# Routed attention and a mixture of experts on one core: the order of the first pair's preparation

## The chip, the core and the metric

The kernel runs on one core of a Trainium2 chip. The core has five engines, each with its own queue that it works through in order: TensorE (PE in the profile, its weight loads PEld), VectorE (DVE), ScalarE (ACT), GpSimd (POOL) and SyncE (SP), which here only starts transfers. ScalarE and GpSimd can start transfers too. Transfers run on 16 DMA engines of the core. SBUF is the working memory; TensorE writes into the banks of PSUM, and VectorE and ScalarE copy results out of them. The metric is the device time of one execution in microseconds; of several executions the median counts.

## What is computed

First attention for 4 batches of 8 heads, 768 tokens and 64 columns a head. Every row of q and k is given to the nearest of 16 centroids of its head, by cosine, and a query sees only the keys with its own centroid. Then a router sends each of the 3072 rows of the attention's output to one of 8 experts, a two-layer network.

```python
q_assign = np.argmax(np.einsum('bhsd,hcd->bhsc', q_n, c_n), axis=-1)
k_assign = np.argmax(np.einsum('bhsd,hcd->bhsc', k_n, c_n), axis=-1)
mask = q_assign[:, :, :, None] == k_assign[:, :, None, :]
scores = np.where(mask, scale * np.matmul(q, k.transpose(0, 1, 3, 2)), -1000000000.0)
attn = softmax(scores)
x = rows_of(np.matmul(attn, v))          # (3072, 512)
logits = xn @ en.T / tau
out[mask_e] = gate_w[mask_e, None] * (np.maximum(x[mask_e] @ w1[e], 0.0) @ w2[e])
```

Here `q_n`, `k_n`, `c_n`, `xn` and `en` (from `expert_emb`) are rows divided by their norm.

## The kernel before

**Tiling.** Two heads of one batch are a pair; there are 16 pairs. A pair has 12 units: two halves of the queries (384 columns) by six blocks of 128 keys. A unit is `scores` (L347 to L361), `expo` (L363 to L366) and `attend` (L368 to L396). `scores` is four matrix products for the two heads into one PSUM tile `s_ps`, of which there are two: first the H part, bf16 one-hot rows of the centroids (`kH` against `qH`, scaled by 2 to the 60th, so that only keys of the query's centroid survive the exponential), then the T part, the float32 rows themselves (`kT` against `qT`). The two parts add up in PSUM. `expo` takes the exponential on ScalarE, which frees the `s_ps` tile. `attend` multiplies with v on TensorE and adds up the denominators on VectorE (`acc`).

**Preparation of a pair.** `prep_pieces` (L228) gives seven pieces. `turn0` and `turn1` transpose one half of q and one of k on TensorE, three 128 by 128 blocks each, into a PSUM bank of `misc` (two banks); ScalarE copies q out (L246, with the scale), VectorE copies k out (L248). `products` multiplies both with the centroids `cnB` (L254) and ScalarE copies the result to `asT` (L262). `assign` turns that (L267); VectorE takes the maximum (L275) and compares (L276), and GpSimd weighs the matches (L277). `choose` (L283, L284) makes one-hot rows `oh` on VectorE. `hots` turns them (L297) and copies them out as `qH` (VectorE, L303) and `kH` (ScalarE, L306); with k's turn goes a small product with `vs` (L320). `values` (L313 to L315) makes `vs`, sums over v, on GpSimd.

**Order.** Inside one block (from L840) the order of TensorE, VectorE and ScalarE is that in which the program is written; the other engines, and what stands ahead of the block, are ordered by the framework's scheduler. In the block all seven pieces of pair 0 come first, then scores and exponentials of units 0 and 1. Then the loop takes two units a round: scores and exponentials of the two units after, then `between` (L798), which puts one piece of the next pair at each of the six rounds `it` of half a pair, then the two attends, and every sixth unit `total` (L397), the sums of the denominators.

**The beginning.** `load` (L136) starts two transfers of 192 KB for each of q, k and v of a pair, all from SP's queue. ScalarE's queue starts those of the centroids, of the experts' rows `emb` and of `tau`. Ahead of the block stand memsets and small constants, then the centroids: `unit_rows` (L194) takes a Square and a Sqrt on ScalarE and two small VectorE instructions; the rows are scaled (L207), turned (L209) and copied to `cnB` (L212). The experts' rows go the same way (L219 to L224) to `embT`, which is first read when the first batch is routed. Pair 1's `turn0` comes in the first round of the loop, its `turn1` after the first two attends (L878).

Of the kernel before, what the change touches and what calls it, by code (L numbers as in the profile page):

```python
# [9 lines left out]
F32 = mybir.dt.float32  # L10
BF16 = mybir.dt.bfloat16
I32 = mybir.dt.int32
ALU = mybir.AluOpType
ACTF = mybir.ActivationFunctionType
# [4 lines left out]
P = 128  # L19
# [18 lines left out]
def kernel(  # L38
# [12 lines left out]
    nc = tc.nc  # L51

    B, H, S, D = q.shape
    C = centroids.shape[1]
    E, DM = moe_expert_emb.shape
# [4 lines left out]
    HS = S // 2  # L60
# [8 lines left out]
    KD = DM // P  # L69
# [15 lines left out]
    ident = const.tile([P, P], F32, name="ident")  # L85
    identb = const.tile([P, P], BF16, name="identb")
    cnB = const.tile([P, NHP, 2 * C], F32, name="cnB")
    embT = const.tile([P, KD, 2 * C], F32, name="embT")
# [3 lines left out]
    epsc = const.tile([P, 1], F32, name="epsc")  # L92
# [22 lines left out]
    smp = ctx.enter_context(tc.tile_pool(name="smp", bufs=2))  # L115
# [14 lines left out]
    def misc():  # L130
        return psM.tile([P, 512], F32, tag="misc", name="misc")
# [1 line left out]
    pairs = [(b, hp) for b in range(B) for hp in range(NHP)]  # L133
    ld = {}

    def load(n, names):  # L136
        b, hp = pairs[n]
        t = ld.setdefault(n, {})
        for nm in names:
            t[nm] = ldp.tile([P, NJ, 2, D], F32, tag=nm + "32", name=nm + "32")  # L140
            for h in range(2):
                nc.sync.dma_start(
                    out=t[nm][:, :, h],
                    in_={"q": q, "k": k, "v": v}[nm][b, 2 * hp + h].rearrange(
                        "(p j) d -> p j d", j=NJ
                    ),
                )

    c_sb = smp.tile([P, D], F32, name="c_sb", bufs=1)
    emb = smp.tile([E, DM], F32, name="emb", bufs=1)  # L150
    tau = smp.tile([E, 1], F32, name="tau", bufs=1)
    load(0, "qkv")
    nc.scalar.dma_start(out=c_sb, in_=centroids.rearrange("h c d -> (h c) d"))
    nc.scalar.dma_start(out=emb, in_=moe_expert_emb)
    nc.scalar.dma_start(out=tau, in_=moe_tau.to_broadcast([E, 1]))


    make_identity(nc, ident)
# [32 lines left out]
        for t in range(2):  # L191
            nc.gpsimd.memset(oh[:, :, 2 * t : 2 * t + 2, :, C : C + 1], (-1.0, 1.0)[t])

    def unit_rows(dst, src, n):  # L194

        junk = smp.tile([P, DM], F32, tag="junk", name="junk")
        nc.scalar.activation(
            junk[0:n, 0 : src.shape[1]], src, ACTF.Square, accum_out=dst
        )
        nc.scalar.activation(dst, dst, ACTF.Sqrt)  # L200
        nc.vector.tensor_scalar(dst, dst, 1e-6, None, ALU.add)
        nc.vector.reciprocal(dst, dst)

    cn_r = smp.tile([P, 1], F32, name="cn_r", bufs=1)
    cn2 = smp.tile([P, 2, D], F32, name="cn2", bufs=1)
    unit_rows(cn_r, c_sb, P)
    nc.vector.tensor_scalar(cn2, bc(c_sb, [P, 2, D], 1), cn_r, None, ALU.mult)  # L207
    bk = misc()
    nc.tensor.transpose(bk[:, 0:P], cn2.rearrange("p a d -> p (a d)"), ident)  # L209
    for par in range(2):  # L210
        rows = slice(D * par, D * par + D)
        nc.vector.tensor_copy(  # L212
            cnB[rows, :, C * par : C * par + C],
            bk[rows, 0:P].rearrange("p (i h c) -> p i h c", h=2, c=C)[:, :, par],
        )

    en_r = smp.tile([E, 1], F32, name="en_r", bufs=1)
    unit_rows(en_r, emb, E)
    nc.vector.reciprocal(tau, tau)  # L219
    nc.vector.tensor_scalar(emb, emb, en_r, tau, ALU.mult, ALU.mult)  # L220
    bk = misc()
    for c in range(KD):
        nc.tensor.transpose(bk[:, E * c : E * c + E], emb[:, P * c : P * c + P], ident[0:E, 0:E])
    nc.vector.tensor_copy(  # L224
        embT[:, :, 0:E], bk[:, 0 : KD * E].rearrange("p (c e) -> p c e", e=E)
    )

    def prep_pieces(n):  # L228

# [4 lines left out]
        def turn(nm, half):  # L234
            if half == 0:
                t[nm + "T"] = trp.tile([P, S], F32, tag=nm + "T", name=nm + "T")
            bk = misc()
            for j in range(NJ // 2):
                nc.tensor.transpose(  # L239
                    bk[:, P * j : P * j + P],  # L240
                    t[nm][:, NJ // 2 * half + j].rearrange("p h d -> p (h d)"),
                    ident,
                )
            dst = t[nm + "T"][:, HS * half : HS * half + HS]
            if nm == "q":
                nc.scalar.activation(dst, bk[:, 0:HS], ACTF.Copy, scale=scale)  # L246
            else:
                nc.vector.tensor_copy(dst, bk[:, 0:HS])  # L248

# [94 lines left out]
    gr = [dict() for _ in range(ngroups)]  # L344
    xr, xT = {}, {}

    def scores(i):  # L347

        n, hq, j = units[i]
        t = ld[n]  # L350
        s_ps = un[i]["s_ps"] = psS.tile([P, 2, 512], F32, tag="s_ps", name="s_ps")
        for l, r, first in (("kH", "qH", True), ("kT", "qT", False)):
            for h in range(2):
                rows = slice(D * h, D * h + D)
                nc.tensor.matmul(  # L355
                    s_ps[:, h, 0:HS],
                    lhsT=t[l][rows, P * j : P * j + P],
                    rhs=t[r][rows, HS * hq : HS * hq + HS],
                    start=first,
                    stop=not first,  # L360
                )  # L361

    def expo(i):  # L363
# [428 lines left out]
    def piece(n, name):  # L792
        if n < NP:
            if n not in prepare:
                prepare[n] = prep_pieces(n)
            prepare[n][name]()

    def between(n, it):  # L798
        b, nb = divmod(n, NHP)
        if it == 5:  # L800
            piece(n + 2, "turn0")
            if n + 1 == NP:
                route[b] = route_pieces(b)
                rows(2 * n)
                route[b][0](0)
        elif it == 0:
            piece(n + 1, "turn1" if n else "turn0")
        elif it == 1:
            piece(n + 1, "values")
            piece(n + 1, "products")  # L810
            if n > 0:
                rows(2 * n - 2)
        elif it == 2:
            piece(n + 1, "assign")
            if n > 0:
                rows(2 * n - 1)
        elif it == 3:
            piece(n + 1, "choose")
        elif it == 4:
            piece(n + 1, "hots")  # L820
        if b > 0:
            if nb == 0 and it == 3:
                route[b - 1] = route_pieces(b - 1)
                for half in range(2):
                    route[b - 1][0](half)
            j = NJ * nb + it - 3
            if 0 <= j < NJ:
                route[b - 1][2](j)
            if nb == 1 and it == 3:
                for half in range(2):  # L830
                    route[b - 1][1](half)
            if nb in (1, 2) and 0 <= j - NJ < 4:
                route[b - 1][3][j - NJ]()
        if b == B - 1 and (nb, it) in early:
            early[nb, it]()
        if b == B - 1 and (nb, it) == (3, 0):
            weights(0)
            weights(1)

    with tc.manual_schedule(engines={EngineType.PE, EngineType.DVE, EngineType.Activation}):  # L840
        for name in ("turn0", "turn1", "values", "products", "assign", "choose", "hots"):
            piece(0, name)
        load(1, "qk")
        for m in range(2):
            scores(m)
            expo(m)
        for i in range(0, len(units), 2):
            n, it = divmod(i // 2, NJ)
            if it == 0 and n + 1 < NP:
                load(n + 1, "v")  # L850
            if it == 4 and n + 2 < NP:
                load(n + 2, "qk")
            if it == 0 and n == 1:

                for w in range(2):
                    nc.sync.dma_start(
                        out=w1s[w], in_=moe_w1[0].rearrange("(c p) f -> p c f", p=P)
                    )
                    nc.sync.dma_start(
                        out=w2s[w], in_=moe_w2[0].rearrange("(c p) d -> p c d", p=P)  # L860
                    )
            for m in range(i + 2, min(i + 4, len(units))):
                scores(m)
                expo(m)
            between(n, it)
            if i % GU == 2 and i > GU:
                divide(i // GU - 1)
            if i + 2 == len(units):
                ats.close()
                tile_waits = {"side": "right", "reuse_waits": "tile"}  # L870
                psX = ctx.enter_context(tc.tile_pool(name="psX", bufs=1, space=PSUM, **tile_waits))
                turn_x(0, nc.scalar.copy, xp.tile([P, DM], F32, tag="acc", name="xTm"))
            for m in range(i, i + 2):
                attend(m)
            if i % GU == 0 and i > 0:
                total(i // GU - 1)
            if i == 0:
                piece(1, "turn1")  # L878
        at.close()
        mop = ctx.enter_context(tc.tile_pool(name="mop", bufs=2, **tile_waits))  # L880
        rtb = ctx.enter_context(tc.tile_pool(name="rtb", bufs=1, **tile_waits))
# [113 lines left out]
```

## Time and profile before

| | us |
|---|---|
| median of 7 runs | 857.1 |
| lowest and highest of them | 856.34, 858.3 |
| the profiled execution's own time | 855.15 |
| its span, first to last instruction | 853.4 |
| mean granted clock of TensorE over the span | 0.993 |

The page has a line for each engine with its busy time; then the span cut into slices; then the chain of work that ended last, followed back from the last instruction to what released it; and the costliest groups of instructions, with the line of the kernel, the tiles they write and read, and how long their engine sat idle before them. The timeline lists instructions by start and length. The view by windows gives, for a stretch of time, the busy time of each engine, the share of TensorE's clock that was granted, and the rate of the transfers. Times in these views count from the start of the span. A float32 product shows as two instructions, so a unit's scores are two bf16 instructions and four float32 ones.

Some lengths, from the timeline, that the steps below use:

| instruction | us |
|---|---|
| L142 starting two transfers, on SP | 1.34 to 1.41 |
| L153, L154, L155 starting one transfer each, on ScalarE | 0.38, 0.78, 0.28 |
| ACT_TABLE_LOAD on ScalarE | 1.28 |
| L246, L248, L262, copy out of PSUM, 128x384 | 0.49, 0.56, 0.48 |
| L275, L276 on 128x384 | 0.56, 0.56 |
| L277 on GpSimd, at 15.24 and at 36.26 | 0.91, 1.56 |
| L366 exponential of a unit | 0.81 |

### The profile page before, as it was taken

How to read it: one execution, taken by the hardware profiler on the slowest of the kernel's cores; microseconds unless marked ns; L12 is line 12 of the kernel's file. 1: busy time of each engine (PE TensorE's matmuls, PEld its weight loads, DVE VectorE, ACT ScalarE, POOL GpSimd, SP SyncE). 2: the span in 40 equal slices, each digit the busy share in tenths (PEclk: the TensorE clock that was granted, in tenths of full speed). 3: DMA queues.
4: the chain of work that ended last, by engine and by line, in shares of the span. 5: the costliest groups of instructions: out<-in, count | busy, mean ns of one | idle time of the engine just before them, and what ended most of it. 6: DMA issues, size and time to landing. Idle time of an engine off the chain costs nothing.

```text
span 853.4 us, 12807 instructions
## 1 busy us (share of the span) xinstructions
PE 826.2 (97%) x5227; PEld 490.7 (58%) x5227; DVE 362.6 (42%) x521; ACT 305.6 (36%) x489; POOL 126.6 (15%) x172
## 2 busy tenths in 40 slices
PE   4999999999999999999899999999999999999995
PEld 2444444444444444444386767667676767767672
DVE  3577878787878877789935000000000000000000
ACT  3555556755567555665451111111111111111110
POOL 4010111211112111021101101010110101010100
PEclk9999999999999999999999999999999999999998
DMA  9922211252211522011127847748393847216410
GB/s 235 338 64 57 56 33 24 57 131 56 56 32 25 130 56 57 20 38 57 38 100 297 299 168 270 281 150 314 128 332 128 301 162 274 95 47 252 183 38 22
DMA packets 108781, 115.24 MB, mean 135 GB/s; under 512 B 77221, under 2 KB 77221, under 8 KB 108208
## 3 DMA queue, kind: packets, MB, share of 16 engines
q1 hardware_dynamic: 104064, 100.68, 37.4%
q0 software_dynamic: 4480, 13.65, 4.3%
q8 instruction: 43, 0.70, 0.3%
q14 instruction: 18, 0.15, 0.1%
q10 hardware_dynamic: 176, 0.05, 0.0%
HBM read 152.11 MB, written 13.64 MB: 194 GB/s over the span
## 4 chain that ended last, share of the span: by engine, by line
PE 51%; issue 25%; DMA 20%; DVE 2%; POOL 0%; SPq 0%; ACT 0%; POOLq 0%; ACTq 0%
PE s_ps L355 19%; DMA out_dram<-y,sidx 17%; PE o_ps L375 16%; PE misc L239 3%; PE h_ps L739 3%; DMA out_dram<-y,gidx 3%; PE misc L402 2%; PE y_ps L755 2%; PE misc L436 2%; PE misc L297 1%; PE misc L254 1%; PE misc L267 1%; PE misc L458 1%; DVE den L411 1%; DMA v<-in_v_dram 1%
## 5 line engine op out<-in xcount | busy, mean ns | idle before, releaser
L739 PEld LDWEIGHTS h_ps<-xTm,w1s 128*128 128x128 f32 x1792 | 202.5, 192 | 24.4 <-DVE xTm L727 20.4
L739 PE MATMUL h_ps<-xTm,w1s 128*128 128x128 f32 x1792 | 207.9, 277 | 2.9 <-DMA w1s<-in_moe_w_dram 2.0
L755 PE MATMUL y_ps<-w2s,hT 128*128 128x512 f32 x448 | 201.1, 592 | 0.0
L366 ACT ACTIVATE prob<-s_ps 128x768 f32<-128x768 f32 x192 | 154.0, 811 | 124.3 <-PE s_ps L355 97.7
L727 DVE COPY xTm<-x_ps 128x512 f32<-128x512 f32 x24 | 16.6, 692 | 333.2 <-PE x_ps L725 333.2
L355 PE MATMUL s_ps<-qT,kT 64*128 64x384 f32 x768 | 157.2, 488 | 0.0
L375 PE MATMUL o_ps<-prob,v 128*64 128x384 f32 x768 | 145.1, 499 | 0.0
L394 DVE TENSOR_TENSOR acc<-acc,prob 128x768 f32<-128x768 f32 x128 | 129.8, 1014 | 3.6
L755 PEld LDWEIGHTS y_ps<-w2s,hT 128*128 128x128 f32 x448 | 81.0, 190 | 81.8 <-issue 81.8
L746 ACT ACTIVATE hT<-h_ps 128x512 f32<-128x512 f32 x56 | 33.4, 597 | 201.5 <-PE h_ps L739 201.5
L411 DVE RECIPROCAL den<-den 128x384 f32<-128x384 f32 x32 | 81.7, 2552 | 31.1 <-ACT den L410 31.1
L355 PEld LDWEIGHTS s_ps<-qT,kT 64*128 64x128 f32 x768 | 69.8, 192 | 22.2 <-issue 22.2
L375 PEld LDWEIGHTS o_ps<-prob,v 128*64 128x64 f32 x768 | 46.6, 136 | 53.9 <-issue 53.0
L765 ACT ACTIVATE y<-y_ps,xin 128x512 f32<-128x512 f32 x28 | 19.2, 687 | 150.3 <-PE y_ps L755 139.1
L766 POOL DMA_INDIRECT out_dram<-y,sidx x24 | 24.1, 1003 | 292.2 <-ACT y L765 286.3
L355 PE MATMUL s_ps<-qH,kH 64*128 64x384 bf16 x384 | 64.3, 332 | 0.9 <-ACT kH L306 0.9
L355 PEld LDWEIGHTS <-kH 64*128 64x128 bf16 x384 | 19.0, 94 | 70.4 <-issue 47.7
L313 POOL TENSOR_TENSOR vs<-v 128x384 f32<-128x384 f32 x16 | 16.2, 1012 | 205.2 <-DMA v<-in_v_dram 194.5
L277 POOL TENSOR_TENSOR sel<-sel,prefc 128x384 bf16<-128x384 bf16 x16 | 24.3, 1516 | 107.2 <-DVE sel L276 107.2
L695 POOL DMA_INDIRECT xin<-x_rows,gidx x28 | 29.7, 1062 | 32.3 <-issue 12.4
L248 DVE COPY kT<-misc 128x384 f32<-128x384 f32 x32 | 17.8, 557 | 36.7 <-PE misc L239 36.7
L384 DVE SCALAR_TENSOR_TENSOR acc<-prob 128x768 f32<-128x768 f32 x32 | 30.3, 947 | 0.0
(183 smaller groups left out, 496.7 us busy)
## 6 DMA issues: line engine op xcount, KB each, us to landing
w1s<-in_moe_w_dram SPq DMA_DIRECT2D x30, 2048.0 KB
w2s<-in_moe_w_dram SPq DMA_DIRECT2D x30, 2048.0 KB
x_rows<-xr SPq DMA_DIRECT2D x4, 1539.0 KB
q<-in_q_dram SPq DMA_DIRECT2D x32, 192.0 KB
k<-in_k_dram SPq DMA_DIRECT2D x32, 192.0 KB
v<-in_v_dram SPq DMA_DIRECT2D x32, 192.0 KB
xin<-x_rows,gidx POOLq DMA_INDIRECT x28, 7.3
out_dram<-y,sidx POOLq DMA_INDIRECT x24, 6.9
```

Of the source, the lines that this page charges most:

```text
L239: nc.tensor.transpose(bk[:, P * j : P * j + P], t[nm][:, NJ // 2 * half + j].rearrange("p h d -> p (h d)"), ident,)
L277: nc.gpsimd.tensor_tensor(sel, sel, bc(prefc, shp, 1), ALU.mult)
L355: nc.tensor.matmul(s_ps[:, h, 0:HS], lhsT=t[l][rows, P * j : P * j + P], rhs=t[r][rows, HS * hq : HS * hq + HS], start=first, stop=not first,)
L366: nc.scalar.activation(d["prob"], d["s_ps"][:, :, 0:HS], ACTF.Exp)
L375: nc.tensor.matmul(g["o_ps"][D * h : D * h + D, 0:HS], lhsT=ld[n]["v"][:, j, h], rhs=d["prob"][:, h], start=(j == 0), stop=(j == NJ - 1),)
L384: nc.vector.scalar_tensor_tensor(out=g["acc"], in0=un[i - 1]["prob"], scalar=NJ * EPS, in1=d["prob"], op0=ALU.add, op1=ALU.add,)
L394: nc.vector.tensor_tensor(g["acc"], g["acc"], d["prob"], ALU.add)
L411: nc.vector.reciprocal(d["den"], d["den"])
L695: nc.gpsimd.indirect_dma_start(out=xin, out_offset=None, in_=x_rows[0:n], in_offset=bass.IndirectOffsetOnAxis(ap=gidxs[part][:, c : c + 1] ...
L739: nc.tensor.matmul(bk[:, m : m + P], lhsT=w1s[j % 2][:, c, f0 + m : f0 + m + P], rhs=d["xT"][:, P * c : P * c + P], start=(c == 0), stop=( ...
L746: nc.scalar.activation(d["hT"][:, f0 : f0 + 512], bk, ACTF.Relu)
L755: nc.tensor.matmul(bk, lhsT=d["hT"][:, P * c : P * c + P], rhs=w2s[j % 2][:, c], start=(c == 0), stop=(c == KF - 1),)
```

## The change

All of it concerns what runs before and during the first pair.

The transfers: pair 0's k is started from ScalarE's queue, behind the centroids and ahead of `emb` and `tau`; on SP q of pair 0 is followed by q and k of pair 1, and only then by v of pair 0. The norms are split into `norm_rows` (ScalarE) and `inverse` (VectorE). The turns of the centroids and of the experts' rows become functions: the first is called after both turns of q and k of pair 0, the second in round 3 of pair 0, behind `choose` of pair 1. The experts' Square and Sqrt come after `products` of pair 0, followed by an exponential of a single column whose result nothing reads. `scores` can do its T part alone first and its H part later. The T parts of units 0 and 1 stand between `choose` and `hots` of pair 0, with pair 1's `turn0` between them; that turn's k is copied out by ScalarE instead of VectorE. Pair 1's `turn1` moves ahead of the first two attends.

```diff
-    load(0, "qkv")
     nc.scalar.dma_start(out=c_sb, in_=centroids.rearrange("h c d -> (h c) d"))
+    load(0, "q")
+    load(0, "k", nc.scalar)
     nc.scalar.dma_start(out=emb, in_=moe_expert_emb)
     nc.scalar.dma_start(out=tau, in_=moe_tau.to_broadcast([E, 1]))
+    load(1, "qk")
+    load(0, "v")
...
-    def unit_rows(dst, src, n):
+    def norm_rows(dst, src, n):
         junk = smp.tile([P, DM], F32, tag="junk", name="junk")
         nc.scalar.activation(
             junk[0:n, 0 : src.shape[1]], src, ACTF.Square, accum_out=dst
         )
         nc.scalar.activation(dst, dst, ACTF.Sqrt)
-        nc.vector.tensor_scalar(dst, dst, 1e-6, None, ALU.add)
-        nc.vector.reciprocal(dst, dst)
+    def inverse(norm):
+        nc.vector.tensor_scalar(norm, norm, 1e-6, None, ALU.add)
+        nc.vector.reciprocal(norm, norm)
...
+    def turn_experts():
+        inverse(en_r)
+        nc.vector.reciprocal(tau, tau)
+        nc.vector.tensor_scalar(emb, emb, en_r, tau, ALU.mult, ALU.mult)
+        bk = misc()
+        for c in range(KD):
+            nc.tensor.transpose(
+                bk[:, E * c : E * c + E], emb[:, P * c : P * c + P], ident[0:E, 0:E]
+            )
         nc.vector.tensor_copy(
+            embT[:, :, 0:E], bk[:, 0 : KD * E].rearrange("p (c e) -> p c e", e=E)
         )
...
             if nm == "q":
                 nc.scalar.activation(dst, bk[:, 0:HS], ACTF.Copy, scale=scale)
+            elif (n, half) == (1, 0):
+                nc.scalar.copy(dst, bk[:, 0:HS])
             else:
                 nc.vector.tensor_copy(dst, bk[:, 0:HS])
...
-    def scores(i):
+    def scores(i, parts="HT", first=True, last=True):
...
         elif it == 0:
-            piece(n + 1, "turn1" if n else "turn0")
+            piece(n + 1, "turn1")
...
         elif it == 3:
             piece(n + 1, "choose")
+            if n == 0:
+                turn_experts()
...
-        for name in ("turn0", "turn1", "values", "products", "assign", "choose", "hots"):
-            piece(0, name)
-        load(1, "qk")
+        piece(0, "turn0")
+        piece(0, "turn1")
+        turn_centroids()
+        piece(0, "products")
+        norm_rows(en_r, emb, E)
+        nc.scalar.activation(warm, epsc, ACTF.Exp)
+        piece(0, "assign")
+        piece(0, "choose")
+        piece(0, "values")
+        scores(0, "T", last=False)
+        piece(1, "turn0")
+        scores(1, "T", last=False)
+        piece(0, "hots")
         for m in range(2):
-            scores(m)
+            scores(m, "H", first=False)
             expo(m)
...
-            if i == 0:
-                piece(1, "turn1")
```

## The prediction

> **What bounds the kernel now.** I read the page first, then the chain of waits over the first 40 us, then the timeline of that stretch engine by engine, then busy time and granted clock in windows.
>
> ```profile
> span 853.4 us, 12807 instructions
> PE 826.2 (97%) x5227; PEld 490.7 (58%) x5227; DVE 362.6 (42%) x521; ACT 305.6 (36%) x489; POOL 126.6 (15%) x172
> ```
>
> TensorE is the bound, and the table of waits lists no PE wait at all between 26 and 400 us. So what a change of the beginning is worth is how much earlier PE reaches its unbroken stretch, less whatever it adds inside that stretch. The chain of the beginning (start, length, what):
>
> ```profile
> 4.25 4.37 DMA v<-in_v_dram
> ...
> 15.24 0.92 POOL sel L277
> ...
> 16.18 0.56 DVE pm L283
> ...
> 16.77 0.75 DVE oh L284
> ...
> 17.66 0.95 PE misc L297 x12
> ...
> 18.97 0.81 ACT kH L306
> ...
> 19.82 5.97 PE s_ps L355 x24
> 25.80 0.80 PE misc L239 x6
> ...
> 28.85 1.72 PE s_ps L355 x12
> ```
>
> The first score starts at 19.82, after the masks of pair 0. The four score units then take 5.97 us, 1.49 each; at 28.85 two units (x12) take 1.72, 0.86 each. Why, the windows show (window: length, busy PE, PEld, DVE, ACT, POOL, granted clock, DMA share, GB/s):
>
> ```profile
> 7.96:11.37 3.41, 3.06 (x15) 2.21 (x18) 1.16 (x4) 0.98 (x2) 1.99 (x5) 1.00 1.33 217
> 11.37:14.79 3.42, 2.04 (x12) 0.56 (x11) 1.30 (x3) 0.48 (x1) 0.00 (x0) 1.00 1.30 217
> 14.79:18.20 3.41, 0.54 (x10) 0.57 (x11) 1.68 (x4) 0.00 (x0) 2.80 (x4) 1.00 1.17 281
> 18.20:21.61 3.41, 2.52 (x16) 1.64 (x14) 0.70 (x2) 2.08 (x2) 0.16 (x1) 0.50 1.02 401
> 21.61:25.02 3.41, 3.41 (x16) 2.01 (x16) 0.00 (x0) 1.79 (x3) 0.00 (x0) 0.50 1.04 384
> ```
>
> The clock falls to 0.50 at 18.2, after a window with PE 16% busy, and returns at 25.02, after a full one; 74% busy did not lift it, 60% busy did not lower it. Before 11.37 the view prints 1.00 only because no change is recorded: three turns of q take 0.87 at 8.31 and 0.55 at 25.73, so it was half there too.
>
> Last, the place where the change puts the experts' turn, it == 3 of pair 0:
>
> ```profile
> 36.10 2.53 DVE L394 TENSOR_TENSOR acc<-acc,prob 128x768 f32<-128x768 f32 x2
> 38.56 0.54 DVE L283 TENSOR_REDUCE pm<-sel 128x24 bf16<-128x384 bf16 x1
> 39.13 0.56 DVE L284 TENSOR_TENSOR oh<-sel,pm 128x384 bf16<-128x384 bf16 x1
> ```
>
> PE's attend of unit 6 starts at 38.09 there, while DVE is busy until 39.69.
>
> **Part 1: the start up to the masks.** Before, the first turn of q stood at 8.31 behind the centroids' and experts' turns and their two PSUM banks, not behind data. Six 192 KB transfers land by 8.62 (the end of v's wait); at 218 GB/s one is 0.90 us, so q was there at 5.0 and k at 6.8.
>
> k now goes through ScalarE's queue. Its issues there were 0.38 (c_sb), 0.78 (emb) and 0.28 (tau); k adds two of 0.67 (SP's rows: 1.34 for two), so they end near 3.65 instead of 2.26. Behind them: table load 1.28, Square and its accumulator 0.35, table load 1.28, Sqrt 0.20: 6.8. DVE's norm, reciprocal and cn2 took 0.67 (6.09 to 6.76): 7.55, and the eight small casts behind them 0.8: 8.35. Arrival is bounded by two readings: both queues share 218 GB/s with pair 1's q behind q (q 6.5, k 7.1), or k does not slow q (q 5.0, k 6.2). I take the first, since two windows in a row at 217 GB/s look like a ceiling.
>
> The Trainium skill, "DMA: Bandwidth & Descriptors", section "Issuing engines are not separate DMA queues", says that transfers started by different engines run on the same 16 DMA engines and that a second issuer saves only issue time. It speaks against a gain from the second queue; by it the sum uses q 6.5 and k 7.1, without it 5.0 and 6.2, and the sum comes out the same.
>
> Turns: q half 0 from 6.5 to 7.4, k half 0 to 8.05, its eviction 0.56 from 8.35 (casts), q half 1 to 8.85, k half 1 from 8.95 to 9.85, eviction done 10.45 (before 11.97). Earlier data moves only the first of these; ACT (6.8) and DVE (8.35) hold the rest. Then the centroids' two copies to cnB, 0.45 with their gaps: 10.95. Products: 0.85 at full clock (30.50 to 31.35), 1.7 at half: done 11.9 to 12.7, before 12.86. From products to the hots' turns nothing changes: 12.86 to 17.66 is 4.8. Hots at 16.7 to 17.5. From there to the end of kH: 1.06 (41.89 to 42.95) plus 0.80 at full clock, 2.11 measured mostly at half. kH ends at 18.5 to 19.5; I take 18.95 (before 19.77).
>
> **Hidden on the way.** v becomes the tenth transfer instead of the sixth: 8.62 + 4 x 0.90 = 12.2, and POOL's three sums (1.00, 0.46, 0.46) end at 14.2. sel is ready near 14.1 to 14.9, so they hide whether POOL has them ahead of sel or behind it; bounds 0 to +0.5. SP's later loads (q and k of pair 2, the weights) come earlier by the two k issues and the earlier turns; no PE wait depends on them. ACT after asT (12.4 to 13.2): Square and accumulator 0.7, Sqrt 0.2, the warming Exp with its table load 1.5, two evictions of pair 1 0.97: done 15.8 to 16.6, before the hots need these banks. Whether Square after Sqrt needs a reload no row shows: 0, or two loads, 2.57. The nearest row is Copy after Sqrt (L246 at 9.22), which has none: 0.
>
> **Part 2: the gap.** PE was idle from 13.98 to 17.63. Into it go the T part of units 0 and 1 (0.65 each at full clock, 28.95 to 29.60; 1.28 at half, 20.12 to 21.40) and pair 1's turn0 (0.80, or 1.5): 2.1 at full clock, 4.05 at half. From 13.3 this ends at 15.4 or 17.4, by the time of the hots. The windows are then well filled, so I expect full clock by kH.
>
> After kH, by rows at full clock: H of unit 0, first exp possible 0.42 later, exp 0.81; unit 2 needs its bank (1.28 to 2.14 after kH), unit 3 to 3.0, turn1 0.81, two attends 1.44: 5.25 after kH, at 24.2. The same work stood done at 28.85. **Gain 4.65** (5.1 to 4.1 over the range of kH).
>
> **Part 3: the experts' turn in the stream.** The preamble's four small turns move behind choose of pair 1. PE, DVE and ACT keep the written order. DVE must finish the two adds, pm and oh (39.69 on before's clock), then add, reciprocal, reciprocal of tau and the scaling of emb: about 0.18 + 0.10 + 0.16 + 0.53, together 1.0. PE comes to the turns at 38.12 and waits until 40.7: 2.55. The turns themselves were 0.59 at half clock; 0.35 taken. Behind them queue attend(6), attend(7) and total(0); nothing downstream has slack, since PE waits nowhere. **Loss 2.9**; bounds 0.35 (emb ready in time) and 4.6 (the stall also costs a window of half clock, 1.7).
>
> The Trainium skill, "TensorE: Matmul & The Clock Gate", section "Part 1: The HAM clock gate", says a wholly idle window of about 3.4 us takes the clock down. By it a stall of 2.55 costs no clock: 855.35; this trace leaves 16% to 60% busy open, and a window holding the whole stall is 25% busy: 857.05 if that is enough.
>
> **Sum.** 4.65 - 2.9 = 1.75. The profiled execution took 855.15 for a span of 853.4 and becomes 853.4; it lies 2 below the median 857.1 of the seven runs, from which I subtract: **855.35**.
>
> **Rivals.**
> A, the forecast: 855.35, own range 854.3 to 856.6. Chance 0.50 (0.30 of it faster, 0.20 within the bound).
> B, no stall: emb is ready when PE comes, only 0.35 remains: 857.1 - 4.65 + 0.35 = 852.8. For it: the two adds take 1.94 elsewhere (44.38) against 2.53 here. Against: that recovers 0.6 of 2.55, and pm cannot pass the adds in DVE's queue. 0.18, faster.
> C, the stall lowers the clock for one window: +1.7, 857.05; or two reloads on ACT keep the banks from the hots for 1.3 to 2: 856.6 to 857.4. For it: the 25%. Against: Copy's row, and most phases split the stall over two windows. 0.18 (0.15 within the bound, 0.03 slower).
> D, slower: the clock stays at half through the first four units, because waits (for k, for the masks, for the first exps) leave every window under the 74% that did not lift it. If it returns at 25.0 as before: kH 19.75, units 2 and 3 at 1.6 each to 24.4, turn1 to 25.5, attends to 26.95; gain 1.9, less 2.9: 858.1; one window later 859.8. It decides from a return later than 23. Against: the gap now holds up to 4 us of PE work. 0.14 (0.09 slower by the bound, 0.05 within).
>
> **Numbers.** A measurement here can tell about 0.2%, 1.7 us. Faster 0.30 + 0.18 = 0.48, within 0.20 + 0.15 + 0.05 = 0.40, slower 0.03 + 0.09 = 0.12. The range, 852.6 to 858.3, takes in B and the near case of D.
>
> **What would show it.** Right: first q turn near 6.5; kH ending near 19; first exp before 20; clock 1.00 from before 20; a PE wait of about 2.5 us on DVE's emb ahead of attend of unit 6. Wrong: no such wait (B); a window at 0.50 after it, or table loads at the second Square (C); 0.50 beyond 23 (D); POOL's sums of v between DVE's sel and POOL's sel would make my zero for v wrong.

## The result and the profile after

| | before | after |
|---|---|---|
| median, us | 856.64 (35 runs) | 860.0 (14 runs) |
| lowest and highest | 855.0, 858.57 | 857.27, 862.02 |
| the profiled execution, us | 855.15 | 858.55 |
| its span | 853.4 | 856.5 |

The changed kernel is slower: its time over that of the kernel before is 1.0037, with an interval of 1.0029 to 1.0046. The two profiled executions differ by 3.40 us, about as much as the medians (3.36), and each lies 1.5 below its median, so they can be set against each other.

The page after has the same work in it, but not at the same times:

```profile
span 856.5 us, 12809 instructions
PE 829.3 (97%) x5227; PEld 490.9 (57%) x5227; DVE 362.2 (42%) x520; ACT 306.4 (36%) x491; POOL 126.5 (15%) x172
```

PE issues as many instructions as before, 5227, and is busy 3.1 us longer (829.3 against 826.2). The chain of waits of the beginning (start, length, what) shows where:

```profile
12.69 1.01 POOL vs L328
...
14.71 1.00 POOL vs L328
...
16.32 0.46 POOL vs L330
16.77 0.88 POOL sel L292
17.68 0.56 DVE pm L298
18.26 0.57 DVE oh L299
...
18.97 0.83 PE misc L312 x12
...
20.00 0.81 ACT kH L321
...
26.14 1.72 PE s_ps L371 x12
```

Before, the chain went from DVE's `sel` straight to POOL's `sel` at 15.24. Now six sums of v stand in POOL's queue ahead of it: those of pair 0, and from 14.71 those of pair 1 too, which the scheduler had put behind it before. `kH` ends at 20.80, before at 19.77. The rest of the beginning is shorter all the same: the scores that started at 28.85 start at 26.14, a gain of 2.71.

The table of PE's waits from 26 to 400 us, empty before, now has one line:

```profile
PE misc L233 <- DVE emb L230: 2.5, 1, 2.5
```

That is the experts' turn in round 3. The timeline around it (start, length, engine, line):

```profile
36.42 0.56 DVE L299 TENSOR_TENSOR oh<-sel,pm 128x384 bf16<-128x384 bf16 x1
...
37.31 0.53 DVE L230 TENSOR_SCALAR emb<-emb,en_r,tau 8x512 f32<-8x512 f32 x1
37.90 0.41 PE L233 MATMUL misc<-ident,emb 8*128 8x8 f32 x4 [2.46 <-DVE emb L230]
38.24 2.77 PE L391 MATMUL o_ps<-prob,v 128*64 128x384 f32 x8
```

Before, the same two attends, and the scores behind them, stood here:

```profile
38.09 1.51 PE L375 MATMUL o_ps<-prob,v 128*64 128x384 f32 x8
...
40.17 0.34 PE L355 MATMUL s_ps<-qH,kH 64*128 64x384 bf16 x2
```

The two attends behind the turn took 1.51 before and take 2.77 in the changed kernel, and the scores behind them start late:

```profile
42.02 0.34 PE L371 MATMUL s_ps<-qH,kH 64*128 64x384 bf16 x2
```

The windows say why (window: length, busy PE, PEld, DVE, ACT, POOL, granted clock, DMA share, GB/s):

```profile
34.93:38.34 3.41, 0.95 (x10) 0.42 (x8) 2.81 (x7) 1.38 (x2) 0.18 (x1) 1.00 1.06 376
38.34:41.76 3.42, 3.42 (x12) 1.12 (x12) 1.05 (x2) 0.00 (x0) 0.00 (x0) 0.50 0.84 174
...
406.98:410.39 3.41, 1.24 (x10) 0.38 (x8) 3.17 (x12) 0.81 (x1) 0.04 (x1) 1.00 0.00 0
410.39:413.81 3.42, 3.42 (x14) 1.44 (x12) 3.42 (x4) 0.92 (x2) 0.31 (x1) 0.50 0.00 0
```

The window that holds the stall has PE 28% busy, and in the next the clock is halved. The scores behind it start at 42.02, against 40.17 before: the gain of 2.71 has become a loss of 1.85. The last two rows repeat this near 410 us. There PE waits 2.17 us for `acc` in both kernels. In the profile before, the wait lay across two windows, 66% and 71% busy, and nothing followed:

```profile
403.93:407.35 3.42, 2.25 (x15) 0.68 (x12) 3.11 (x13) 0.81 (x1) 0.00 (x0) 1.00 0.00 0
407.35:410.76 3.41, 2.41 (x16) 1.02 (x16) 3.38 (x6) 1.82 (x3) 0.36 (x1) 1.00 0.00 0
```

Here one window took most of it (36% busy), and 1.6 us more are lost: the attend at 426.51 before stands at 429.97 after. That the profile before has no half clock there is its luck: of the thirteen profiles without extra work at this place, ten have it.

### The profile page after: what moved, and what is told of

It is laid out like the page before. It is cut to its first block, busy times and chain, and to the rows that moved or that the text cites. A ratio compares the mean times of both kernels' runs of the same rounds, so it can differ in the third digit from the quotient of the medians.

```text
span 856.5 us, 12809 instructions
## 1 busy us (share of the span) xinstructions
PE 829.3 (97%) x5227; PEld 490.9 (57%) x5227; DVE 362.2 (42%) x520; ACT 306.4 (36%) x491; POOL 126.5 (15%) x172
## 4 chain that ended last, share of the span: by engine, by line
PE 48%; issue 24%; DMA 22%; DVE 2%; POOL 1%; SPq 0%; ACT 0%; POOLq 0%; DVEq 0%
PE s_ps L371 18%; DMA out_dram<-y,sidx 17%; PE o_ps L391 15%; PE misc L251 3%; DMA out_dram<-y,gidx 3%; PE misc L418 3%; PE h_ps L755 2%; DMA w1s<-in_moe_w_dram 2%; PE misc L452 2%; PE misc L269 1%; PE misc L312 1%; PE misc L282 1%; PE y_ps L771 1%; DVE acc L410 1%; PE misc L474 1%
## 5 line engine op out<-in xcount | busy, mean ns | idle before, releaser
L755 PEld LDWEIGHTS h_ps<-xTm,w1s 128*128 128x128 f32 x1792 | 202.5, 192 | 24.1 <-DVE xTm L743 20.4
L426 ACT COPY den<-misc 128x384 f32<-128x384 f32 x32 | 15.3, 479 | 45.6 <-PE misc L418 45.6
```

The lines of the kernel that those rows point to most:

```text
L755: nc.tensor.matmul(bk[:, m : m + P], lhsT=w1s[j % 2][:, c, f0 + m : f0 + m + P], rhs=d["xT"][:, P * c : P * c + P], start=(c == 0), stop=( ...
```

## The experiments

**The stall in round 3.** First the changed kernel with the experts' part taken out of round 3: scaled behind `assign` of pair 0, turned ahead of `hots` of pair 0.

```diff
         piece(0, "assign")
+        scale_experts()
         piece(0, "choose")
...
         scores(1, "T", last=False)
+        turn_experts()
         piece(0, "hots")
...
             piece(n + 1, "choose")
-            if n == 0:
-                turn_experts()
```

> The changed kernel, but the experts' rows are scaled on VectorE right after pair 0's assign and turned on TensorE behind the second T part, in the start-up gap, so nothing of them is left in round 3 of pair 0. Theory 1 (the loss sits at the experts' turn: 2.46 us of wait, 0.41 of turns, and one window of half clock behind it, 1.7): the profile shows no PE wait between 26 and 400 us, the round-3 attend of unit 6 follows the scores at once, and the time falls from 860.0 by 2.9 to 4.6, to 855.4 to 857.1; against before (856.6) between -2.7 us and +0.5, ratio 0.997 to 1.0005. Rival (the loss is in the start-up itself or in clock windows that fall anywhere): stays above 859, ratio 1.003.

Measured: 856.13, ratio to before 0.9989 (0.9975 to 1.0003); the wait in round 3 is gone. So the late turn costs 0.48% (1.0037 less 0.9989), 4.1 us, more than stall and turn together (2.87). What is left of the change is no gain that can be told from nothing.

The same part put alone into the kernel before:

```diff
-    unit_rows(en_r, emb, E)
...
+    def turn_experts():
+        nc.vector.tensor_scalar(en_r, en_r, 1e-6, None, ALU.add)
...
             piece(n + 1, "choose")
+            if n == 0:
+                turn_experts()
```

> The kernel before with one part of the change alone: the experts' scaling and turns moved into round 3 of pair 0, behind choose of pair 1 (Square and Sqrt stay at the beginning). Theory 1: a PE wait of about 2.5 us on emb in round 3, plus 0.4 of turns, less at most 0.4 won at the first turn of q, plus up to 1.7 of clock: 2.5 to 4.2 us slower than before, ratio 1.003 to 1.005. Rival (the round absorbs it): within 0.5 us of before.

Measured: 859.89, ratio 1.0042 (1.0027 to 1.0056), 3.6 us. Its profile has the stall, 2.45. It fell across a window 84% and one 44% busy, and the second was enough: the granted clock is 0.50 from 41.21 to 44.62. One part of the change, by itself, makes the kernel as much slower as the whole change does.

To tell the stall from its clock, the stall was kept and filled with 18 turns of the identity that nothing reads:

```diff
     def turn_experts():
...
+        bk = misc()
+        for _ in range(18):
+            nc.tensor.transpose(bk[:, 0:P], ident, ident)
         bk = misc()
```

> The changed kernel with 18 turns of the identity (0.13 to 0.14 us each at full clock, 2.4 in all) put on TensorE ahead of the experts' turns in round 3; their result is not read. The stall keeps its length but TensorE is busy in it. Theory 1 with clock (a window mostly idle costs a window of half clock, 1.7): no 0.50 after round 3, the time falls by as much of 1.7 as executions lose to it, 858.3 to 859.5, and the spread of the executions shrinks. Rival (the clock is not tied to this idle time): 860.0 and a 0.50 window still in the profile.

Measured: 859.16, ratio 1.0021 (1.0009 to 1.0033). No window behind round 3 is at half clock, and the attends are back to 1.51:

```profile
37.70 2.18 PE L233 MATMUL misc<-ident 128*128 128x128 f32 x18
...
40.63 1.51 PE L394 MATMUL o_ps<-prob,v 128*64 128x384 f32 x8
```

From 1.0037 to 1.0021 is 1.4 us for the clock, near the 1.7 of one window; the intervals overlap, so the size is rough.

This kernel begins exactly as the changed one, and its profile shows how much the beginning depends on where the windows fall. One window, from 16.98, took much of PE's wait for the masks and that for `kH`; it is 29% busy, and the next two are at half clock:

```profile
16.98:20.39 3.41, 1.00 (x14) 0.95 (x14) 1.67 (x3) 0.68 (x1) 0.36 (x1) 1.00 1.00 382
20.39:23.80 3.41, 2.65 (x12) 1.37 (x14) 0.16 (x1) 1.64 (x4) 0.00 (x0) 0.50 1.03 400
```

The scores behind the first two attends start at 28.47 here: of the gain of 2.71 only 0.38 is there.

**The masks.** The weighing of pair 0's matches on VectorE instead of GpSimd, so that no sum of v can stand ahead of it:

```diff
-            nc.gpsimd.tensor_tensor(sel, sel, bc(prefc, shp, 1), ALU.mult)
+            weigh = nc.vector if n == 0 else nc.gpsimd
+            weigh.tensor_tensor(sel, sel, bc(prefc, shp, 1), ALU.mult)
```

> The changed kernel with one instruction moved: pair 0's weighing of the matches (sel times prefc) runs on VectorE instead of GpSimd, where it stood behind both pairs' sums over v and began 1.45 us after its input. Theory 2a (GpSimd's queue held the masks, and behind it TensorE's gap work at half clock is the next bound, its second T part ending at 18.36): the hots' turns begin near 18.4 instead of 18.97, the time falls by 0.6 us to 859.4. Theory 2b (GpSimd's queue alone set the masks): hots near 17.4, time down by 1.45 or more, 858.5. Either way the wait of 2.5 us at the experts' turn stays, and the kernel stays slower than before.

Measured: 858.58, ratio 1.0021 (1.0010 to 1.0032). `oh` is done at 17.10 instead of 18.82, but the hots come at 18.41, only 0.56 earlier. PE's timeline shows what holds them now:

```profile
13.99 1.65 PE L372 MATMUL s_ps<-qT,kT 64*128 64x384 f32 x4
15.57 0.90 PE L251 MATMUL misc<-ident,q 128*128 128x128 f32 x3
...
17.04 1.44 PE L372 MATMUL s_ps<-qT,kT 64*128 64x384 f32 x4
18.41 0.84 PE L313 MATMUL misc<-identb,oh 128*128 128x128 bf16 x12
```

It is the gap's own work at half clock: T parts of 1.65 where full clock takes 0.92. Two waits lay side by side, GpSimd's and the clock's, and taking one away shows the other. The time fell by 1.4 us, of which the hots explain 0.56; the intervals of this kernel and the changed one overlap, and the rest is open.

Both moves together, the matches on VectorE and the experts early (the two diffs above):

> The changed kernel with both repairs: the experts' rows scaled and turned in the start-up gap, and pair 0's weighing on VectorE. Theory (the two places are separate: round 3 costs 2.9 us and clock, the masks 0.5 to 1.45): the hots' turns begin at 18.4 if the gap's TensorE work runs at half clock and near 17 if it runs at full clock, no wait in round 3; the time falls from 860.0 by 4.1 (the move alone) and a further 0.5 to 1.4: 854.4 to 855.4, ratio to before 0.997 to 0.9985. Rival (the move alone already gave all there is, the clock then falls in the first units): as the move alone, ratio 0.999.

Measured: 854.58, ratio 0.9975 (0.9962 to 0.9988). The first version under the kernel before, by 2.1 us, still less than half of what the prediction had for the beginning.

Pair 0's k back on SyncE's queue:

```diff
-    load(0, "k", nc.scalar)
+    load(0, "k")
```

> The changed kernel with k of pair 0 started from SP's queue behind q, as before the change; the rest as changed. Theory (both queues share one rate, and ScalarE's and VectorE's first steps hide the arrival): q lands 1.0 to 1.4 us earlier and k within 0.5 of before, ScalarE's norms come 1.3 earlier, the turns end up to 1 us earlier, and the masks are still held by GpSimd's sums over v (v lands as before near 12.5): the time stays within 0.7 us of 860.0. Rival (the second queue is worth an arrival): 1 us or more slower than the changed kernel.

Measured: 857.33, ratio 1.0030 (1.0015 to 1.0045), not to be told from the change's 1.0037. q is turned at 5.49 instead of 6.35 and k at 7.28 instead of 7.55, so the second queue made both later. The Trainium skill, "DMA: Bandwidth & Descriptors", section "Issuing engines are not separate DMA queues", has a second issuer save only issue time; here it did not bring even an earlier arrival. The median, 2.67 below the changed kernel's, says little. The runs fall into two groups, six of 856.57 to 857.33 and five of 859.93 to 861.39. And here the scheduler put POOL's `sel` ahead of the second sums, so that this kernel tests two things at once. The profile, one of the first group, shows the beginning when the masks are not held and the clock is back early (full from 16.57):

```profile
15.07 0.91 POOL L292 TENSOR_TENSOR sel<-sel,prefc 128x384 bf16<-128x384 bf16 x1 [0.34 <-DVE sel L291]
...
15.94 0.99 POOL L328 TENSOR_TENSOR vs<-v 128x384 f32<-128x384 f32 x1
```

`kH` ends at 19.42 and the scores behind the first two attends start at 24.75, 4.10 earlier than before. The stall in round 3 and two windows of half clock, behind it and near 410 us, then take more than that back.

**The clock.** The kernel before, with 25 turns of the identity in the gap of 3.68 us ahead of its hots, and nothing else:

```diff
             piece(0, name)
+            if name == "assign":
+                bk = misc()
+                for _ in range(25):
+                    nc.tensor.transpose(bk[:, 0:P], ident, ident)
```

> The kernel before with 25 turns of the identity on TensorE between pair 0's assign and its hots, where it sat idle from 13.98 to 17.63; their result is not read. Theory (much of what the change could win in the start-up is the clock, which falls because of this gap): the clock stays at 1.00 past 18.2, the first four score units take 0.86 us each or wait for exponentials, and the time falls by 1.5 to 2.8, to 853.8 to 855.1, ratio 0.997 to 0.998. Rival (the first units are held by the masks and exponentials, not by the clock): within 0.5 of 856.6.

Measured: 853.48, ratio 0.9963 (0.9949 to 0.9977): work that nothing reads makes the kernel 3.2 us faster. The windows:

```profile
14.70:18.12 3.42, 2.45 (x27) 2.24 (x26) 1.77 (x3) 0.00 (x0) 2.72 (x4) 1.00 1.20 282
18.12:21.53 3.41, 2.35 (x21) 1.39 (x19) 0.72 (x2) 2.79 (x3) 0.26 (x1) 1.00 1.00 394
```

The window from 14.70 has PE 72% busy instead of 16%, and the clock stays. The hots start when they did (17.68); units 0 and 1 take 0.82 each instead of 1.49, and the first attend comes at 24.22 instead of 26.53.

The version with both moves, plus such turns at four places of the beginning, the last of them directly behind `products`; `keep_busy(n)` issues n turns of the identity into a PSUM tile that nothing reads:

```diff
+        keep_busy(20)
         piece(0, "turn0")
+        keep_busy(3)
         piece(0, "turn1")
         turn_centroids()
+        keep_busy(5)
         piece(0, "products")
+        keep_busy(3)
```

> The same with TensorE kept busy by turns of the identity into a spare PSUM bank that nobody reads: 20 ahead of the first turn of q, 3 between turn0 and turn1, 5 ahead of products, 3 behind it. Theory (the rest of the start-up's price is the clock): the clock is at 1.00 before 9 us and stays there; products 0.85, T parts 0.92 each, hots near 16.5, end of kH near 18, first attend near 22 instead of 24.63; time 5 us under before, 851.0 to 852.5, ratio 0.993 to 0.995. Rival (VectorE's and ScalarE's chain to the masks sets the start whatever the clock): hots after 18, ratio 0.997 or more.

Measured: 854.42, ratio 0.9979 (0.9971 to 0.9988), as without them, and not the 0.993 to 0.995 expected. From 4.3 to 18 us everything runs at full clock and is done sooner. Then PE has less to do before the masks come: the window from 14.57 is 54% busy, and the two from 17.98 on run at half. The idle time had only moved. The masks were held too: `emb`'s scaling, 1.21 here, stands between `sel`, done at 14.28, and `pm`, which starts at 15.76, and the hots come at 17.24.

The kernel with the filled gap, with 14 turns more ahead of the `total` near 404 us:

```diff
     def total(g):
...
         bk = misc()
+        if g == ngroups - 3:
+            for _ in range(14):
+                nc.tensor.transpose(bk[:, HS : HS + P], ident, ident)
```

> The kernel before with its first gap filled, and 14 turns of the identity also ahead of the total of group 29, where PE waits 2.2 us near 404 us for acc and the clock then stands at 0.50 for one window in most profiles. Theory (a window under about 55% busy costs the next 3.4 us half the clock, wherever it stands): no 0.50 window near 407, 1.0 to 1.7 us less than with the first gap filled alone: ratio to before 0.9940 to 0.9955. Rival (the clock matters only at the beginning): as with the first gap filled alone, 0.9963 plus or minus 0.0005, or more by the turns' own 1.2 us.

Measured: 853.86, ratio 0.9968 (0.9956 to 0.9979), no better than without, against 0.9940 to 0.9955 expected. The 0.50 near 407 is gone from the profile, and the 14 turns fit into the wait: the `total` starts 3.68 behind the start of the two attends ahead of it, without the turns 3.67. But this one start of the kernel had half clock until 17.9, which the other had only until 11.3. The 25 turns of the first gap then took 4.43 instead of 2.89 and held the hots until 19.05, against 17.68: a fill that fits at full clock is itself a delay at half clock. That a gain of up to 1.7 in some executions is lost in such a spread is likely, but not shown.

**Order and clock together.** The changed kernel with k on SyncE's queue, the matches of pair 0 on VectorE, the experts scaled behind `choose` of pair 0 and turned behind its hots, and identity turns in every gap of the beginning:

```diff
+        keep_busy(20)
         piece(0, "turn0")
+        keep_busy(3)
         piece(0, "turn1")
         turn_centroids()
+        keep_busy(5)
         piece(0, "products")
+        keep_busy(3)
...
         piece(0, "choose")
+        scale_experts()
...
         scores(1, "T", last=False)
+        keep_busy(10)
         piece(0, "hots")
+        turn_experts()
+        keep_busy(5)
         for m in range(2):
             scores(m, "H", first=False)
             expo(m)
+        keep_busy(7)
```

> The change with all that the runs named put right: k of pair 0 from SyncE again, pair 0's matches weighed on VectorE, the experts scaled behind choose of pair 0 and turned behind its hots, and turns of the identity that nothing reads put into TensorE's gaps of the beginning (20 ahead of the first turn of q, 3, 5 and 3 up to products, 10 ahead of hots, 5 ahead of the H parts, 7 behind them). Theory (order and clock both set the beginning): full clock from the first turn of q on and no 0.50 window before 100 us, kH ends by 19.0, first attend at 22.5 to 23.5 against 26.53 before, no wait in round 3: ratio to before 0.993 to 0.9965. Rival (order alone counts, the fill pays nothing): as the two moves without fill, 0.9975 or above.

Measured: 847.84 (847.6 to 850.11, 4 runs), ratio 0.9895 (0.9877 to 0.9913): 9 us under the kernel before, more than expected. The chain of its beginning has PE, and hardly any wait, from 11.5 on:

```profile
11.50 0.55 PE misc L284 x3
12.05 0.85 PE s_ps L374 x4
...
14.70 1.24 PE spare L865 x10
15.94 0.35 PE misc L315 x6
```

The hots start at 15.78, `kH` ends at 17.62, the first attend comes at 21.84, 4.69 earlier than before, and the scores behind the first two attends at 23.35, 5.50 earlier. The profiled executions differ by 5.04 (850.11 against 855.15), although this one loses 1.6 again to a half-clock window at 403 us; behind 430 us it is 1.2 shorter than the one before, and no run says why. The other 4 us are only argued: the profiled execution is the slowest of the four, and the means of the granted clock of the other three (0.997 and 0.998 against 0.995) speak for no such window; and the median of the kernel before lies 2 above its own profile.

The same with the 14 turns ahead of `total`, by the diff already shown:

> Both together: the order put right, the fill of the beginning, and the 14 turns ahead of the total of group 29. Theory: the two gains add up, ratio to before 0.9915 to 0.995, below each of the other two kernels of this set. Rival (one of the two fills costs as much as it saves): no better than the better of the other two.

Measured: 848.94 (4 runs), ratio 0.9907 (0.9889 to 0.9926). The profile has no 0.50 between 5 and 841 us, and the time is no better. The intervals overlap, with four runs each; that the two gains add up, as expected, is not shown.

Then order and fill apart. The order alone, the version of 847.84 without any identity turn:

```diff
-        keep_busy(20)
         piece(0, "turn0")
-        keep_busy(3)
...
         turn_experts()
-        keep_busy(5)
...
-        keep_busy(7)
```

> The order put right (k from SyncE, pair 0's matches weighed on VectorE, the experts scaled behind choose of pair 0 and turned behind its hots) without any turns of the identity. Theory (order and clock share the gain): kH ends by 19.5, but at least one window of the first 30 us stands at 0.50 and the first attend comes at 23.5 to 25.5 against 21.84 with the fill: ratio to before 0.993 to 0.997. Rival (the order is all of it): as with the fill, 0.9895 plus or minus 0.002, first attend by 22.5.

Measured: 855.32, ratio 0.9974 (0.9961 to 0.9988). Its profiled execution is a good one, full clock from 17.22 on and the first attend at 23.31. Of its 12 runs four took 851.25 to 852.64 and eight 855.2 to 855.7; the time lost by the mean clock (one less the clock, times the span) is 1.7 to 4.3 us in the four and 6.0 to 6.8 in the eight. This counts the idle end of the kernel too, and not what comes ahead of the clock's first record.

The fill alone, in the changed kernel as it is (up to `products` as above):

```diff
         scores(1, "T", last=False)
+        keep_busy(20)
         piece(0, "hots")
+        keep_busy(8)
...
             expo(m)
+        keep_busy(7)
```

> The changed kernel as it is, with turns of the identity in TensorE's gaps of the beginning alone (20 ahead of the first turn of q, 3, 5 and 3 up to products, 20 ahead of hots, 8 behind them, 7 behind the H parts). Theory: with the clock held the first units cost 0.86 instead of 1.3 to 1.6, but the masks still wait for GpSimd and the experts' turn still stops PE 2.5 us in round 3: kH ends at 19.5 to 20.5, first attend at 23.0 to 24.2 against 24.63, ratio to before 0.998 to 1.002, against 1.0037 unfilled. Rival (the fill is most of the 9 us): ratio 0.993 or below. Rival (fill pays nothing here): 1.003 or above.

Measured: 857.39, ratio 1.0012 (0.9999 to 1.0024). From 6.26 on all of the beginning runs at full clock, so that GpSimd's order stands bare in the timeline:

```profile
13.28 0.56 DVE L291 TENSOR_TENSOR sel<-misc,amax 128x384 bf16<-128x384 f32 x1
...
14.49 1.00 POOL L328 TENSOR_TENSOR vs<-v 128x384 f32<-128x384 f32 x1
...
16.52 0.92 POOL L292 TENSOR_TENSOR sel<-sel,prefc 128x384 bf16<-128x384 bf16 x1
...
18.76 0.83 PE L312 MATMUL misc<-identb,oh 128*128 128x128 bf16 x12 [1.13 <-DVE oh L299]
```

`sel` is ready at 13.84 and waits until 16.52 for sums that TensorE first reads at 19.43 (pair 0's) and in round 4 (pair 1's). The hots come at 18.76, hardly before the change's 18.97; with the order mended as well they come at 15.78. So the fill alone is worth 0.25% and the order alone 0.63%, of which 0.48% is the experts' turn by the first experiment; together, with somewhat fewer turns around the hots, they are worth 1.42% (1.0037 to 0.9895). Each hides what the other would give.

## Why the prediction was wrong

It had 855.35, 1.75 under the kernel before; it became 3.4 over. The stages of the profile, in its own terms:

| term | predicted | measured |
|---|---|---|
| Gain, at the scores behind the first two attends | 4.65 | 2.71 |
| Loss, stall and turns | 2.9 | 2.87 |
| the stall's clock | 0 taken, bound 1.7 | 1.7 |
| the same wait near 410 us, now in one window | not in the sum | 1.6 |

The measured column adds up to 3.46 more than before at 430 us, as the attend there shows; the two spans differ by 3.1 and the two executions by 3.40, so some 0.3 is won back behind it.

**What bounds the kernel** was right: PE had no slack behind the beginning, and each stall there reached the end.

**Part 1** held up to the products: the first turn of q at 6.35 (forecast 6.5), k's evictions done at 10.57 (10.45), products done at 12.59, the half-clock end of 11.9 to 12.7. (In it 6.8 and 0.67 make 7.47, not 7.55; nothing hangs on the difference.) It failed at "from products to the hots' turns nothing changes": 4.8 became 6.4, and `kH` ended at 20.80 instead of 18.95.

**The step that failed** in the beginning is Hidden on the way: "they hide whether POOL has them ahead of sel or behind it; bounds 0 to +0.5". The sums meant there were pair 0's, and they did end in time (14.75 for a forecast of 14.2). Overlooked was that POOL's order is the scheduler's and that pair 1's three sums, 2.07 us more, could come ahead of `sel` too. In the change they held `sel` 1.46 us (15.27 to 16.73), with the clock held 2.7 (13.84 to 16.52). That Square needs no table load behind Sqrt was right.

With it failed Part 2's "this ends at 15.4 or 17.4, by the time of the hots". The gap's work ended at 18.36: it began at 14.01 instead of 13.3, and a T part took up to 1.65 at half clock, not 1.28. Of the time by which the hots came late, 18.97 against 16.7 to 17.5, GpSimd's order alone accounts for only 0.56, as the matches on VectorE show; the gap's work would have held them until 18.4 in any case.

**Part 2**, from `kH` on: "5.25 after kH" was right, 5.34 measured; nearly all of the missing gain (1.94) is the time of `kH`, 1.85 late. "I expect full clock by kH" came true in this execution only in the letter: the clock rose at 17.86, near the end of the gap's work, which took 4.35, more than the 4.05 of half clock. In other starts (the experts early, the stall filled) PE's wait for the masks took it down again near 20.4, so that 2.71 is itself a good case. At the place where the sum has 4.65, the gain was 4.10 with k on SyncE's queue, where the scheduler's order and the windows happened to fall well, and 5.50 with order and clock both held. So the working from `kH` to the scores was sound, and the premises on GpSimd's order and on the clock were not.

**Part 3**: place and cause of the stall were right, and its size to a tenth (2.46 against 2.55). Here the second step failed, the stall's clock: zero was taken and one full window came, 1.7, as rival C had it; a window 28% busy was enough. C itself, at 857.05, missed the rest, since it kept the whole Gain. In "most phases split the stall over two windows" lay the mistake: in the kernel before with the experts late, the stall was split, and its second half was still enough. Rival D's return of the clock behind 23 did not occur in this profile, but it did in the profile with the stall filled, whose beginning is the same (27.21, with a gain of 0.38 where D had 1.9). So D describes the clock of some executions. B's missing stall did not occur.

The Trainium skill, "TensorE: Matmul & The Clock Gate", section "Part 1: The HAM clock gate", has the clock go down after an idle window; the rows here put it down after windows in which PE was 16 to 57% busy. The free-running window of 3.4 us, which it states as well, is what the rows show (3.413).

## What to carry to other kernels

A wait of 2.5 us on TensorE may cost 4: look at how much of the 3.4-us windows around it stays filled, and fill the rest with turns that nothing reads, or move the late instruction. Fill no more than fits at half clock, where the same turns take longer. A step moved to another place must be followed into the queues whose order is not written by hand; whatever can now start earlier may be put ahead of what matters. When two causes lie side by side, an experiment on each alone shows little, and only the one with both tells what they are worth.

## What the runs showed of the hardware

How the clock went can be read from the windows of the fifteen profiles, leaving out each kernel's idle end. A window at full clock was followed by half clock 21 times, with PE 16 to 57% busy in it; no window above 57% was, and none under 47% was without. In between both occur. Half clock was lifted after windows 84 to 100% busy, and not lifted after any under 84% (nor after two, of 87 and 90%). This takes what stands ahead of the clock's first record as half clock, as the lengths of the turns there suggest; inside the record it was lifted after 96 to 100%. The grid of windows stands differently to the start of the kernel from profile to profile (a window begins at 14.45 in the changed kernel, at 13.56 with the stall filled), which fits that one kernel's times fall into groups, 3 to 4 us apart in the order alone.

VectorE's scaling of `emb` took 0.53 us in round 3 and 1.23 where it ran beside GpSimd's sums of v (the experts early):

```profile
14.57 1.00 POOL L330 TENSOR_TENSOR vs<-v 128x384 f32<-128x384 f32 x1
14.62 1.23 DVE L230 TENSOR_SCALAR emb<-emb,en_r,tau 8x512 f32<-8x512 f32 x1
```

It took 1.21 in the version with both moves and the clock held, 0.79 and 0.80 where only a part of it ran beside such sums (both moves; order and clock together), and 0.53 again in the order alone, with GpSimd idle. With the experts early alone this cost the masks nothing, since `pm` waited for POOL's `sel` until 17.57; with the matches on VectorE it stood between `sel` and `pm`. Scaled behind `choose` it delays nothing.
